# A three-stage float32 kernel: the experts' token tiles go from 512 to 768, and the MLP's output is prepared in single steps

## The chip, the cores and the metric

The kernel runs on one core of a Trainium2 chip. The metric is the device time of one execution in microseconds (us); smaller is better. The engines of the core are TensorE (PE, matrix products into PSUM, with weight loads listed apart as PEld), VectorE (DVE), ScalarE (ACT), GpSimd (POOL) and SyncE (SP), which here does nothing but issue the transfers (DMA) between DRAM and the on-chip buffer. TensorE's granted clock has two levels, 1.2 and 2.4 GHz; views write it as a share of full speed, 0.50 to 1.00.

## The reference

Three stages follow each other, on 4 x 576 = 2304 tokens of width 512:

```python
# 1: linear attention, 4 batches x 8 heads x 576 x 64, features of 128
proj = q_or_k @ w_phi;  proj -= max|proj|;  phi = concat(exp(proj), exp(-proj))
x = (phi_q @ (phi_k^T v)) / (phi_q . sum(phi_k) + 1e-6)      # -> 2304 x 512
# 2: MLP, 512 -> 2048 -> 512
h = x @ w_in
x = (h * clip(h + 3, 0, 6) / 6) @ w_out
# 3: eight experts, 512 -> 1024 -> 512, every token through every expert
P = exp(x @ w_gate - max); 8 times: P /= row sums; P /= column sums; P *= 2304 / 8
out = sum over e of P[:, e] * (relu(x @ w1[e]) @ w2[e])
```

## The kernel before, in words

**Number format.** A float32 operand is split into a rounded high half and the rest, the low half. A product is three matmuls into the same PSUM bank: high by high, low by high, high by low (`mm3`, lines 80 to 82). The two halves are made by one operation each: `hi_act` (ACT, line 67) and `lo_dve` (DVE, line 73), or `hi_pool` and `lo_pool` (POOL, lines 70 and 76).

**Order.** The program is written as Python generators that are advanced in turn. A scheduler in the framework then reorders the instructions within each engine when the kernel is built. Every engine runs its own list in order, and a wait for another engine or a transfer holds whatever stands behind it in that list. SP's list is that of all transfers.

**Attention and MLP.** The tokens are cut into chunks of 512, the last of 256. The MLP runs in four groups: chunks 0, 1 and 2 alone, then chunks 3 and 4 together. `mlp(g)` yields once for each step, and the attention of later batches is woven between the steps. In a step the first product goes to the bank `ps_h` (or `ps_kv` for chunk 4); ACT makes `t`, DVE makes `u`, ACT and DVE make the halves `gh` and `gl`, and the second product adds into the accumulators. Those are the banks `ps_acc`, and for chunk 4, whose 256 tokens need half as much, the two `ps_att` banks.

**The MLP's output.** Stage 3 multiplies its first layer by Strassen's scheme (seven products of half size in place of eight). The scheme's seven operands on the token side are `b11`, `b22`, `b21` (quarters of the transposed MLP output) and the differences `t1` to `t4`. When a group ends, `quarters()` copies the accumulators out (ACT, line 470, tile `xf`), makes four differences on POOL (line 476, tile `xt`), and `x_out()` makes the halves of each operand (tile `xo`, two buffers) and writes them to DRAM (line 463, `xs_...`). All of this stands at the end of the group in one piece. The buffers of `xf` and `xt` are those named `raw`, `t` and `u` of the pool `cv`, which the MLP's steps use too. Chunk 4 is not split in seven: its two operands `k1` and `k2` are read straight from `ps_att` by ACT and DVE.

**Experts.** A block is one expert and one half of its hidden layer; there are 16. For each block the five chunks pass through. A chunk of 512 takes the seven products in the order t1, b11, b22, t2, b21, t3, t4, each 4 x 3 matmuls of 256 columns in a half bank (`product`); the last chunk takes the full product, 48 matmuls of 256 columns. After a product ACT copies it (`kept`, line 785, tile `u`), or DVE adds a kept one to it (`plus`, line 789), and `relu_halves` makes the two halves of a hidden tile `h` (lines 762 and 763). `outputs()` is the second layer: 12 matmuls of 512 columns for each 128 tokens, of the chunk before, woven in by `PATTERN`. So a block has 4 x 84 + 48 = 384 matmuls of 256 columns and 18 x 12 = 216 of 512.

Operand tiles return from DRAM into `xr` (five buffers, asked for five products ahead by `x_ahead`, line 637). Expert weights land in `raw2` (8 buffers, lines 575 and 581), and POOL makes from them eight operands `w1o` a block (12 buffers) and four `w2o` (6 buffers). In views and in the order below the names are shortened: `raw` also stands for `raw2`, and all transfers of weights for `in_moe_w_dram`.

Of the kernel before, what the change touches and what calls it, by code (L numbers as in the profile page):

```python
# [21 lines left out]
def tile_kernel(ctx: ExitStack, tc, q, k, v, w_phi, w_in, w_out, w_gate, w1, w2, out):  # L22
# [81 lines left out]

    xctx = ctx.enter_context(ExitStack())
# [10 lines left out]
    def x_cols(c0, c1):  # L116
# [7 lines left out]
    HF = CH // 2  # L124
    XOPS = ("b11", "b21", "b22", "t4", "t1", "t2", "t3")
    xs = [
        {o: dram.tile([P, 4 * HF], F32, name="xs_%d_%s" % (ci, o)) for o in (XOPS if n == CH else ("k1", "k2"))}
        for ci, (_, n) in enumerate(chunks)
    ]
# [15 lines left out]
    def convert(dst, src):  # L145
        raw = cv.tile([P, DM, 2], I32, tag="raw", name="raw")
# [39 lines left out]
    xe = mctx.enter_context(tc.tile_pool(name="xe", bufs=1))  # L186
# [211 lines left out]
    def mlp(g):  # L398
# [60 lines left out]
    def x_out(ci, name, src):  # L459
        t = xe.tile([P, 2, 2, HF], F32R, tag="xo", name="xo", bufs=2)  # L460
        hi_act(t[:, 0], src)
        lo_dve(t[:, 1], src, t[:, 0])
        nc.sync.dma_start(xs[ci][name], f32(t).rearrange("p h k t -> p (h k t)"))

    def quarters(ci, o):
        q = []
        for h in range(2):
            f = cv.tile([P, 2, CH], F32, tag="raw", name="xf")
            for k in range(2):
                nc.scalar.copy(f[:, k], o[2 * h + k])  # L470
            q += [f[:, :, 0:HF], f[:, :, HF:]]
        b11, b12, b21, b22 = q

        def sub(a, b, tag):
            t = cv.tile([P, 2, HF], F32, tag=tag, name="xt")
            nc.gpsimd.tensor_tensor(out=t, in0=a, in1=b, op=ALU.subtract)
            return t

        t1 = sub(b12, b11, "t")
        t2 = sub(b22, t1, "u")  # L480
        for name, src in (("t1", t1), ("b11", b11), ("b22", b22), ("t2", t2), ("b21", b21)):
            x_out(ci, name, src)
        x_out(ci, "t3", sub(b22, b12, "t"))
        x_out(ci, "t4", sub(b21, t2, "u"))
# [84 lines left out]
    def w_load(b):  # L569
        e, j = blocks[b]  # L570
        for r in range(2):
            for k in range(2):
                t = wp.tile([P, 2, BF], F32, tag="raw2", name="raw2", bufs=8)
                src = w1[e, k * HF:(k + 1) * HF, r * FH + j * BF:r * FH + (j + 1) * BF]
                nc.sync.dma_start(t, src.rearrange("(k p) f -> p k f", p=P))
                raw[b, "a%d%d" % (r + 1, k + 1)] = t
        for r in range(2):
            for q in range(QB):
                t = wp.tile([P, DM], F32, tag="raw2", name="raw2", bufs=8)
                f0 = r * FH + j * BF + q * P  # L580
                nc.sync.dma_start(t, w2[e, f0:f0 + P, :])
                raw[b, r * QB + q] = t
# [8 lines left out]
    def w1_prep(b):  # L591
        a = {o: raw.pop((b, o)) for o in ("a11", "a12", "a21", "a22")}
# [6 lines left out]
        def keep(o, src):  # L599
            wops[b, o] = halves("w1o", 12, src)  # L600

        s1 = add(a["a21"], a["a22"], ALU.add)
        keep("s1", s1)
        s2 = add(s1, a["a11"], ALU.subtract)
        yield
        keep("s4", add(a["a12"], s2, ALU.subtract))
# [3 lines left out]
        keep("s3", add(a["a11"], a["a21"], ALU.subtract))  # L610
        yield
        for o in ("a11", "a12", "a22", "a21"):
            keep(o, a[o])
            yield

    def w2_prep(b):
        for i in range(2 * QB):
            w2t[b, i] = halves("w2o", 6, raw.pop((b, i)))
            yield
# [6 lines left out]
    ORDER = ("t1", "b11", "b22", "t2", "b21", "t3", "t4")  # L626
    WITH = {"t1": "s1", "b11": "a11", "b22": "s4", "t2": "s2", "b21": "a12", "t3": "s3", "t4": "a22"}
    units = [(b, c) for b in range(len(blocks)) for c in range(len(chunks))]
    wanted = [(c, o) for _, c in units for o in (ORDER if chunks[c][1] == CH else ("k1", "k2"))]
# [3 lines left out]
    def x_ahead(n):  # L633
        while len(xring) < min(n, len(wanted)):
            c, o = wanted[len(xring)]
            t = wp.tile([P, 2, 2, HF], F32R, tag="xr", name="xr", bufs=XR)
            nc.sync.dma_start(f32(t).rearrange("p h k t -> p (h k t)"), xs[c][o])
            xring.append(t)
# [3 lines left out]
    for g in range(len(groups)):  # L642
        im = 0
        s0, s1 = done_by((g + 1) * HP - 1) if g else 0, done_by((g + 2) * HP - 1)
        for _ in mlp(g):
            im += 1
            if g + 1 < B:
                upto(s0 + LEAD + (s1 - s0) * im // (4 * NFF + 1))
            elif im == 8:
                w_load(0)  # L650
                first = w1_prep(0)
            elif im % 8 == 0:
                take(first, 1)
            elif im == 120:
                x_ahead(XR - 1)
# [12 lines left out]
    mo = ctx.enter_context(tc.tile_pool(name="mo", bufs=1, reuse_waits="tile"))  # L668
    hp_ = ctx.enter_context(tc.tile_pool(name="hp", bufs=1, side="right", reuse_waits="tile"))
    acc = mo.tile([P, NTT, DM], F32, name="acc")  # L670
    take(w2_prep(0), 9)
    pm = mo.tile([P, NTT, E], F32, name="pm")

    def sinkhorn():
        r1 = mo.tile([P, NTT], F32, name="r1")
# [28 lines left out]
    def store(i):  # L704
        c = i * P
# [14 lines left out]
    gate_ps = []  # L720
# [210 lines left out]
```

## Time and profile before

| | |
|---|---|
| three timed runs | 2310.23, 2317.01, 2313.9 us; median 2313.9 us |
| profiled execution | 2309.93 us, of which the traced span is 2307.9 us |
| attention and MLP | 0 to about 741 us of the span |
| experts | about 741 us to the end |
| TensorE busy | 2227.2 us, 97% of the span |
| VectorE, ScalarE, GpSimd busy | 48%, 29%, 41% |
| mean granted TensorE clock | 0.988 |

Times are read from the span's start. "Busy" for an engine is the time in which one of its instructions ran. A row in brackets such as `[11.19 <-DVE xo L73]` says that the engine had been idle for 11.19 us and that the DVE instruction of line 73 writing `xo` ended this.

### The profile page before, as it was taken

What the parts mean: (1) busy time and instruction counts of PE and PEld (TensorE: products, weight loads), DVE (VectorE), ACT (ScalarE), POOL (GpSimd) and SP (SyncE); (2) the same over time, 40 slices, a digit from 0 to 9 for tenths busy, and PEclk for the clock granted to TensorE, in tenths of its full rate; (3) what the DMA queues carried; (4) which work ended last, traced back from release to release, by engine and by line L of the source; (5) the groups of instructions that cost most, each with busy time, mean ns of one, the idle gap of its engine ahead of it and who ended that gap; (6) DMA issues with size and microseconds to landing.
All of it is one profiled execution on the core that took longest, in us unless ns stands there. A gap on an engine that the chain in (4) does not pass through costs nothing.

```text
span 2307.9 us, 33330 instructions
## 1 busy us (share of the span) xinstructions
PE 2227.2 (97%) x13207; PEld 1952.3 (85%) x13207; DVE 1105.8 (48%) x1486; ACT 668.3 (29%) x1270; POOL 936.0 (41%) x895
## 2 busy tenths in 40 slices
PE   8899899899899899999999999999999999999999
PEld 6677677788688789899899999999989999899998
DVE  6899876666533215543333433334333343334433
ACT  5566555554322222111121111211112111121111
POOL 2565867776873131623315223142231422314100
PEclk9999999999899899999999999999999999999999
DMA  4354432321511646465465654656546555465464
GB/s 119 100 156 147 143 116 83 111 89 60 214 65 64 225 136 206 160 219 178 165 210 166 213 187 157 210 179 209 186 160 211 180 198 185 163 214 187 156 196 133
DMA packets 181258, 372.42 MB, mean 161 GB/s; under 512 B 70384, under 2 KB 95088, under 8 KB 181104
## 3 DMA queue, kind: packets, MB, share of 16 engines
q1 hardware_dynamic: 181104, 370.29, 48.2%
q8 instruction: 106, 1.74, 0.3%
q14 instruction: 48, 0.39, 0.1%
HBM read 341.39 MB, written 28.84 MB: 160 GB/s over the span
## 4 chain that ended last, share of the span: by engine, by line
PE 66%; DVE 1%; DMA 1%; ACT 0%; issue 0%; ACTq 0%
PE ps_acc L80 11%; PE ps_acc L81 11%; PE ps_acc L82 11%; PE ps_att L80 4%; PE ps_att L82 4%; PE ps_att L81 4%; PE ps_kv L80 3%; PE ps_kv L82 3%; PE ps_kv L81 3%; PE ps_h L80 3%; PE ps_h L82 3%; PE ps_h L81 3%; PE ps_acc L726 0%; DMA xs_b<-xo 0%; DMA xr<-xs_t 0%; PE ps_acc L738 0%
## 5 line engine op out<-in xcount | busy, mean ns | idle before, releaser
L80 PE MATMUL ps_acc<-w2o,h 128*128 128x512 f32 x1152 | 451.8, 392 | 0.0
L81 PE MATMUL ps_acc<-w2o,h 128*128 128x512 f32 x1152 | 451.6, 392 | 0.0
L82 PE MATMUL ps_acc<-w2o,h 128*128 128x512 f32 x1152 | 448.5, 389 | 0.0
L856 DVE SCALAR_TENSOR_TENSOR acc<-ps_acc,pm,acc 128x512 f32<-128x512 f32 x252 | 188.7, 749 | 432.5 <-PE ps_acc L82 431.3
L70 POOL TENSOR_SCALAR w1o<-raw 128x512 fp32r<-128x512 f32 x64 | 46.8, 731 | 646.8 <-PE ps_att L82 643.7
L82 PEld LDWEIGHTS ps_acc<-w2o,h 128*128 128x128 f32 x1152 | 216.6, 188 | 46.9
L80 PEld LDWEIGHTS ps_acc<-w2o,h 128*128 128x128 f32 x1152 | 217.3, 189 | 38.2
L81 PEld LDWEIGHTS ps_acc<-w2o,h 128*128 128x128 f32 x1152 | 217.4, 189 | 35.5
L80 PE MATMUL ps_att<-xr,w1o 128*128 128x256 f32 x768 | 219.1, 285 | 13.1 <-DVE xo L73 11.2
L762 ACT ACTIVATE h<-u 128x512 fp32r<-128x512 f32 x192 | 114.3, 627 | 373.0 <-DVE u L789 373.0
L763 DVE SCALAR_TENSOR_TENSOR h<-u,h 128x512 fp32r<-128x512 f32 x192 | 177.2, 950 | 89.9 <-ACT h L762 89.9
L82 PE MATMUL ps_att<-xr,w1o 128*128 128x256 f32 x768 | 218.7, 285 | 0.0
L81 PE MATMUL ps_att<-xr,w1o 128*128 128x256 f32 x768 | 218.6, 285 | 0.0
L785 ACT COPY u<-ps_att 128x512 f32<-128x512 f32 x128 | 75.1, 587 | 428.8 <-PE ps_att L82 428.8
L80 PE MATMUL ps_kv<-xr,w1o 128*128 128x256 f32 x640 | 181.4, 283 | 0.0
L82 PE MATMUL ps_kv<-xr,w1o 128*128 128x256 f32 x640 | 181.3, 283 | 0.0
L80 PE MATMUL ps_h<-xr,w1o 128*128 128x256 f32 x640 | 181.3, 283 | 0.0
L82 PE MATMUL ps_h<-xr,w1o 128*128 128x256 f32 x640 | 181.3, 283 | 0.0
L81 PE MATMUL ps_h<-xr,w1o 128*128 128x256 f32 x640 | 181.3, 283 | 0.0
L81 PE MATMUL ps_kv<-xr,w1o 128*128 128x256 f32 x640 | 181.3, 283 | 0.0
L76 POOL TENSOR_TENSOR wl<-wf,wh 128x512 fp32r<-128x512 f32 x128 | 174.2, 1361 | 10.2
L80 PEld LDWEIGHTS ps_att<-xr,w1o 128*128 128x128 f32 x768 | 148.1, 193 | 19.5 <-DVE xo L73 11.5
(251 smaller groups left out, 4856.3 us busy)
## 6 DMA issues: line engine op xcount, KB each, us to landing
xr<-xs_t SPq DMA_DIRECT2D x256, 512.0 KB, 4.1
xr<-xs_b SPq DMA_DIRECT2D x192, 512.0 KB, 4.1
raw<-in_moe_w_dram SPq DMA_DIRECT2D x128, 256.0 KB, 3.5
wf<-scratch SPq DMA_DIRECT2D x48, 512.0 KB, 3.2
xr<-xs_k SPq DMA_DIRECT2D x32, 512.0 KB, 3.8
raw<-in_moe_w_in_dram SPq DMA_DIRECT2D x16, 512.0 KB, 3.7
raw<-in_moe_w_out_dram SPq DMA_DIRECT2D x16, 512.0 KB, 3.9
scratch<-wf SPq DMA_DIRECT2D x16, 512.0 KB, 3.1
```

What stands on the lines that cost most here:

```text
L70: nc.gpsimd.tensor_scalar(dst, src, 1.0, 1.0, op0=ALU.mult, op1=ALU.mult)
L76: nc.gpsimd.tensor_tensor(out=dst, in0=src, in1=f32(hi), op=ALU.subtract)
L80: nc.tensor.matmul(o, lhsT=wh, rhs=xh, start=start, stop=False, skip_group_check=chk)
L81: nc.tensor.matmul(o, lhsT=wh, rhs=xl, start=False, stop=False, skip_group_check=chk)
L82: nc.tensor.matmul(o, lhsT=wl, rhs=xh, start=False, stop=stop, skip_group_check=chk)
L762: nc.scalar.activation(t[:, 0], src, AF.Relu)
L763: nc.vector.scalar_tensor_tensor(out=t[:, 1], in0=src, scalar=0.0, in1=f32(t[:, 0]), op0=ALU.max, op1=ALU.subtract)
L785: nc.scalar.copy(t, ps)
L856: nc.vector.scalar_tensor_tensor(out=a, in0=ps, scalar=pm[:, ti, e:e + 1], in1=a, op0=ALU.mult, op1=ALU.add)
```

## The change

**Units.** The experts take the tokens in three units of 768. Of the unit's six tiles of 128 the even ones are one half of Strassen's token side and the odd ones the other. Each of the seven products has two parts, and a part is 6 matmuls of 384 columns in a bank of its own (both `ps_att` banks, or `ps_h` and `ps_kv`). The last 256 tokens are now part of the third unit, and the special case for them (`hidden_last`, `k1`, `k2`) is gone. One `outputs()` follows each of the first six products. A block has 3 x 84 = 252 matmuls of 384 columns and 216 of 512. The gate's matmuls in the first block become 60 of 384 columns instead of 88 of 256.

**The MLP's output.** `operands()` replaces `quarters()` and `x_out()`. At the end of a group it copies the accumulators out (two copies on ACT and two on DVE for a chunk, chunk 4 first) and stops. Each later step makes one operand: differences on DVE instead of POOL, the halves as before, the transfer out one step late and in pieces of one token tile. `make()` takes such a step at every third step of the next MLP group, and two at each part of a product in the first unit of the experts. The tiles lie in a pool `xe` of their own.

**Weights.** Seven `w1o` operands a block instead of eight, in 10 buffers instead of 12; `raw2` has 6 buffers instead of 8, and the loads for the first and the second layer are asked for apart. `h` gets 10 buffers (7 before), `u` 8 (6). The accumulator `acc` of the second layer is opened after the first unit.

```diff
-    HF = CH // 2
-    XOPS = ("b11", "b21", "b22", "t4", "t1", "t2", "t3")
...
+    HK = DM // 2
+    NUN = 3
+    UP = NTT // 2 // NUN
+    UW = UP * P
+    XOPS = ("t1", "b11", "b22", "t2", "b21", "t3", "t4")
+    xs = [{o: dram.tile([P, 4, UW], F32, name="xs_%d_%s" % (c, o)) for o in XOPS} for c in range(NUN)]
...
-        for ci in parts:
-            if chunks[ci][1] == CH:
-                quarters(ci, [rows(ci, dd)[0] for dd in range(KD)])
-            else:
-                for i, o in enumerate(("k1", "k2")):
-                    x_out(ci, o, acc[ci, i].rearrange("p (k t) -> p k t", k=2))
+        for ci in reversed(parts):
+            making.append(operands(ci, rows))
+            next(making[-1])
...
+    def operands(ci, rows):
+        c0, n = chunks[ci]
+        w = n // 2
+        q = {}
         for h in range(2):
-            f = cv.tile([P, 2, CH], F32, tag="raw", name="xf")
+            f = xe.tile([P, 2, 2, w], F32, tag="raw" if n == CH else "xl", name="xf")
             for k in range(2):
-                nc.scalar.copy(f[:, k], o[2 * h + k])
+                src = rows(ci, 2 * h + k)[0].rearrange("p (i s t) -> p s i t", s=2, t=P)
+                dst = f[:, k].rearrange("p s (i t) -> p s i t", t=P)
+                if k == 0:
+                    nc.scalar.copy(dst, src)
+                else:
+                    nc.vector.tensor_copy(dst, src)
...
+        def sub(a, b):
+            t = xe.tile([P, 2, w], F32, tag="xt", name="xt")
+            nc.vector.tensor_tensor(out=t, in0=a, in1=b, op=ALU.subtract)
...
+            t = xe.tile([P, 2, 2, w], F32R, tag="xo", name="xo")
+            hi_act(t[:, 0], q[o])
+            lo_dve(t[:, 1], q[o], t[:, 0])
+            if last is not None:
+                out_(*last)
+            last = o, t
+            yield
...
+    def make(n=1):
+        while n and making:
+            if next(making[0], 1):
+                making.pop(0)
+            n -= 1
...
-                t = wp.tile([P, 2, BF], F32, tag="raw2", name="raw2", bufs=8)
+                t = wp.tile([P, 2 * BF], F32, tag="raw2", name="raw2", bufs=6)
...
-            wops[b, o] = halves("w1o", 12, src)
+            wops[b, o] = halves("w1o", 10, src)
...
             im += 1
+            if im % 3 == 0:
+                make()
...
-    UB, HB = 6, 7
+    UB, HB = 8, 10
...
-    def product(ps, w, x, fresh):
-        for q in range(QB):
-            qs = slice(q * P, (q + 1) * P)
-            o = ps[:, q * HF:(q + 1) * HF]
-            for k in range(2):
-                mm3(o, w[:, 0, k, qs], w[:, 1, k, qs], x[:, 0, k, :], x[:, 1, k, :], fresh and q == 0 and k == 0, True, True)
+    def product(ps, w, x, q, fresh):
+        qs = slice(q * P, (q + 1) * P)
+        for k in range(2):
+            mm3(ps, w[:, 0, k, qs], w[:, 1, k, qs], x[:, 0, k, :], x[:, 1, k, :], fresh and k == 0, True, True)
...
+        for i, o in enumerate(XOPS):
+            x_ahead(n0 + i + XR)
+            x = xring[n0 + i]
             for q in range(QB):
...
+                if o in ("t1", "b21"):
+                    X[q] = bank("att")[:, 0:UW]
+                if o == "b11":
+                    A[q] = bank(("h", "kv")[q])[:, 0:UW]
+                ps = (X if o in ("t1", "b22", "b21") else A)[q]
+                product(ps, wops[b, WITH[o]], x, q, o in ("t1", "b11", "b21"))
...
-    PATTERN = {(7, 0): "UUUUUUU", (7, 4): "UUDUUDUUDUD", (7, 2): "UUDUUUUDU", (2, 4): "UDDUDD"}
...
+        for i, _ in enumerate(hidden(b, c, n0, got)):
+            if not out_pool:
+                make(2)
+            if i % QB == QB - 1 and behind:
                 outputs(*behind.pop(0))
-        n0 += steps
+        if not out_pool:
+            make(99)
+            ectx.close()
+            mo = ctx.enter_context(tc.tile_pool(name="mo", bufs=1, reuse_waits="tile"))
+            out_pool += [mo, mo.tile([P, NTT, DM], F32, name="acc"), mo.tile([P, NTT, E], F32, name="pm")]
+            take(w2_prep(0), 9)
...
         if c == 0:
-            if late is not None:
-                take(late, 2)
+            if b > 0:
+                take(late, 9)
             if b + 1 < len(blocks):
-                w_load(b + 1)
-                coming = w1_prep(b + 1)
-                late = w2_prep(b + 1)
...
-            take(coming, {0: 1, 1: 2, 2: 1, 3: 5, 4: 0}[c])
-            take(late, {1: 1, 2: 1}.get(c, 0))
+                w_load(b + 1, False)
+                coming, late = w1_prep(b + 1), w2_prep(b + 1)
+        if b + 1 < len(blocks):
+            take(coming, (1, 3, 9)[c])
+            if c == 1:
+                w_load(b + 1, True)
+            take(late, (0, 0, 2)[c])
```

How the change moves instructions is seen in three places; lines with - are of the order before, lines with + of the changed one, each a run of instructions as they stand on the engine.

ACT where the MLP's last group ends and the experts begin (`gh` is the last MLP step's, `xf` the copied accumulators, `xo` the operands, `u` the kept products). Before:

```order
L67 ACTIVATE gh<-u 128x256
L470 COPY xf<-ps_acc 128x512 x3
L67 ACTIVATE xo<-xt 128x512
L470 COPY xf<-ps_acc 128x512
L67 ACTIVATE xo<-xf 128x512 x2
L67 ACTIVATE xo<-xt 128x512
L67 ACTIVATE xo<-xf 128x512
L67 ACTIVATE xo<-xt 128x512 x2
L67 ACTIVATE xo<-ps_att 128x512 x2
L785 COPY u<-ps_att 128x512
```

The banks `ps_att` are read last, after all operands of chunk 3. In the changed kernel the same place reads:

```order
L67 ACTIVATE gh<-u 128x256
L472 COPY xf<-ps_acc 128x512 x2
L472 COPY xf<-ps_att 128x256 x2
L67 ACTIVATE xo<-xt 128x256
L67 ACTIVATE xo<-xf 128x256
L804 COPY u<-ps_att 128x384 x2
L804 COPY u<-ps_h 128x384
L67 ACTIVATE xo<-xf 128x256
```

Four copies stand in front of the experts' first work, and the operands are spread behind it.

ACT where the third MLP group ends and the fourth begins (`t` and `gh` are of the new group's steps). Before:

```order
L470 COPY xf<-ps_acc 128x512 x3
L67 ACTIVATE xo<-xt 128x512
L470 COPY xf<-ps_acc 128x512
L67 ACTIVATE xo<-xf 128x512
L436 ACTIVATE t<-ps_h,cst 128x512
L67 ACTIVATE xo<-xf 128x512
L67 ACTIVATE xo<-xt 128x512
L67 ACTIVATE gh<-u 128x512
L436 ACTIVATE t<-ps_kv,cst 128x256
L67 ACTIVATE xo<-xf 128x512
L67 ACTIVATE gh<-u 128x256
```

Every `xo` among these waits for one of two buffers. In the changed kernel:

```order
L472 COPY xf<-ps_acc 128x512 x2
L67 ACTIVATE xo<-xt 128x512
L67 ACTIVATE xo<-xf 128x512
L439 ACTIVATE t<-ps_h,cst 128x512
L439 ACTIVATE t<-ps_kv,cst 128x256
L67 ACTIVATE gh<-u 128x512
L67 ACTIVATE xo<-xf 128x512
L67 ACTIVATE gh<-u 128x256
L67 ACTIVATE xo<-xt 128x512
```

Two operands still stand ahead of the first `t` here, and the others come one or two between the steps.

SP's transfers in the middle of the experts' stage, around the weights of one block (`xr` are operand tiles; the number after `xs_b` or `xs_t` is the operand's). Before:

```order
L637 DMA xr<-xs_t_100 128x1024
L581 DMA raw_9401<-in_moe_w_dram 128x512
L581 DMA raw_9403<-in_moe_w_dram 128x512
L575 DMA raw_10267<-in_moe_w_dram 128x2x256
L637 DMA xr<-xs_b_96 128x1024
L637 DMA xr<-xs_t_101 128x1024
L637 DMA xr<-xs_t_98 128x1024
L575 DMA raw_10269<-in_moe_w_dram 128x2x256
```

In the changed kernel:

```order
L669 DMA xr<-xs_t_101 128x1536
L608 DMA raw_9480<-in_moe_w_dram 128x512
L608 DMA raw_9482<-in_moe_w_dram 128x512
L611 DMA raw_9979<-in_moe_w_dram 128x2x256
L611 DMA raw_9981<-in_moe_w_dram 128x2x256
L669 DMA xr<-xs_b_102 128x1536
```

Four weight loads instead of three now stand together ahead of an operand tile.

## Rows read from the trace of the kernel before

**Rows 1.** The page's head.

```profile
span 2307.9 us, 33330 instructions
```

**Rows 2.** Stretches: length, busy us (instructions) of five engines, clock, DMA share, GB/s.

```profile
276.00:300.00 24.00, 18.11 (x90) 14.05 (x89) 17.19 (x22) 13.31 (x28) 14.68 (x15) 0.93 0.52 173
440.00:466.00 26.00, 20.77 (x99) 16.00 (x98) 18.40 (x24) 15.25 (x30) 18.16 (x16) 0.93 0.47 178
587.00:622.00 35.00, 23.80 (x105) 19.84 (x104) 17.74 (x16) 10.85 (x20) 33.99 (x30) 0.76 0.61 222
741.00:765.00 24.00, 12.80 (x83) 11.83 (x82) 8.14 (x10) 7.20 (x13) 11.53 (x11) 0.72 0.70 263
765.00:2308.00 1543.00, 1535.01 (x9663) 1390.12 (x9663) 593.46 (x829) 295.71 (x501) 441.06 (x426) 1.00 0.55 184
595.00:605.30 10.30, 5.24 (x12) 4.15 (x13) 5.94 (x5) 2.41 (x5) 10.22 (x9) 0.50 0.04 15
612.10:619.00 6.90, 5.16 (x17) 4.46 (x18) 6.52 (x6) 2.72 (x6) 6.90 (x7) 0.51 0.67 254
748.60:762.30 13.70, 6.07 (x27) 5.97 (x28) 3.77 (x6) 4.16 (x7) 7.32 (x8) 0.50 0.63 231
```

**Rows 3.** Timeline of PE in the experts' stage: start, us, instruction.

```profile
1499.89 0.40 PE L80 MATMUL ps_acc<-w2o,h 128*128 128x512 f32 x1
...
1502.64 0.28 PE L80 MATMUL ps_att<-xr,w1o 128*128 128x256 f32 x1
...
1505.51 0.40 PE L80 MATMUL ps_acc<-w2o,h 128*128 128x512 f32 x1
```

**Rows 4.** Timeline of PE in the attention: matmuls of 288 columns.

```profile
293.26 0.29 PE L81 MATMUL ps_att<-El,kvh 128*128 128x288 f32 x1
...
293.79 0.29 PE L82 MATMUL ps_att<-Eh,kvl 128*128 128x288 f32 x1
```

**Rows 5.** Timeline of POOL over one block of the experts.

```profile
1498.70 0.62 POOL L70 TENSOR_SCALAR w1o<-raw 128x512 fp32r<-128x512 f32 x1 [38.38 <-PE ps_att L82]
...
1547.06 0.62 POOL L70 TENSOR_SCALAR w2o<-raw 128x512 fp32r<-128x512 f32 x1 [14.29 <-PE ps_acc L82]
...
1554.40 1.29 POOL L76 TENSOR_TENSOR w2o<-raw,w2o 128x512 fp32r<-128x512 f32 x1
1594.06 0.62 POOL L70 TENSOR_SCALAR w1o<-raw 128x512 fp32r<-128x512 f32 x1 [38.38 <-PE ps_att L82]
```

**Rows 6.** Costliest groups and DMA issues of the page (mean ns; us to landing).

```profile
L763 DVE SCALAR_TENSOR_TENSOR h<-u,h 128x512 fp32r<-128x512 f32 x192 | 177.2, 950 | 89.9 <-ACT h L762 89.9
L785 ACT COPY u<-ps_att 128x512 f32<-128x512 f32 x128 | 75.1, 587 | 428.8 <-PE ps_att L82 428.8
xr<-xs_t SPq DMA_DIRECT2D x256, 512.0 KB, 4.1
```

**Rows 7.** Timelines of ACT, DVE and SP's queue, third to fourth MLP group.

```profile
594.58 0.69 ACT L436 ACTIVATE t<-ps_h,cst 128x512 f32<-128x512 f32 x1 [3.40 <-POOL xt L476]
...
611.17 0.63 ACT L67 ACTIVATE xo<-xf 128x512 fp32r<-128x512 f32 x1 [10.14 <-DMA xs_b<-xo]
...
597.47 1.75 DVE L73 TENSOR_TENSOR xo<-xt,xo 128x512 fp32r<-128x512 f32 x1
...
605.71 0.32 SPq L168 DMA_DIRECT2D wf<-scratch  x1
606.12 0.39 SPq L463 DMA_DIRECT2D xs_b<-xo  x1
```

**Rows 8.** Timelines of DVE and PE where the experts begin.

```profile
755.48 0.69 DVE L73 TENSOR_TENSOR xo<-ps_att,xo 128x512 fp32r<-128x512 f32 x1 [0.65 <-ACT xo L67]
...
756.23 0.58 PE L80 MATMUL ps_att<-xr,w1o 128*128 128x256 f32 x1 [11.19 <-DVE xo L73]
```

**Rows 9.** What PE waited for between 587 and 622 us: total, times, longest.

```profile
PE ps_h L80 <- DVE u L438: 7.0, 1, 7.0
```

More of the change, by code (lines that the diff above doesn't have):

```diff
@@ L623, in take @@
             next(g, 0)
-    ORDER = ("t1", "b11", "b22", "t2", "b21", "t3", "t4")
     WITH = {"t1": "s1", "b11": "a11", "b22": "s4", "t2": "s2", "b21": "a12", "t3": "s3", "t4": "a22"}
-    units = [(b, c) for b in range(len(blocks)) for c in range(len(chunks))]
-    wanted = [(c, o) for _, c in units for o in (ORDER if chunks[c][1] == CH else ("k1", "k2"))]
+    units = [(b, c) for b in range(len(blocks)) for c in range(NUN)]
+    wanted = [(c, o) for _, c in units for o in XOPS]
     XR = 5
@@ L717, in store, with gate_add @@
             c += n
-    gate_ps = []
-    def gate_add(x, kh, tokens, first=False):
+    gate_ps = {}
+    def gate_add(x, kh, t):
+        first = t not in gate_ps
+        if first:
+            gate_ps[t] = bank("acc")
         for k in range(2):
             for h in range(2):
-                for t in tokens:
-                    nc.tensor.matmul(
-                        gate_ps[-1][0:2 * E, t * HF:(t + 1) * HF], lhsT=wg[:, 2 * kh + k, :], rhs=x[:, h, k, :],
-                        start=first and k == 0 and h == 0 and t == tokens[0], stop=True, skip_group_check=True,
-                    )
+                nc.tensor.matmul(
+                    gate_ps[t][0:2 * E, 0:UW], lhsT=wg[:, 2 * kh + k, :], rhs=x[:, h, k, :],
+                    start=first and k == 0 and h == 0, stop=True, skip_group_check=True,
+                )
@@ L731, in gate_end @@
     def gate_end(c):
-        c0, n = chunks[c]
-        lt = hp_.tile([2 * E, CH], F32, tag="u", name="lt", bufs=UB)
-        nc.scalar.copy(lt[:, 0:n], gate_ps.pop(0)[0:2 * E, 0:n])
+        lts = []
+        for t in range(2):
+            lts.append(hp_.tile([2 * E, UW], F32, tag="u", name="lt", bufs=UB))
+            nc.scalar.copy(lts[-1], gate_ps.pop(t)[0:2 * E, 0:UW])
         yield
-        ps = bank("acc")
-        for i in range(n // P):
-            nc.tensor.matmul(ps[:, i * E:(i + 1) * E], lhsT=lt[:, i * P:(i + 1) * P], rhs=sel, start=True, stop=True)
@@ L785, in kept, with plus @@
+        def kept(name, q, ps):
+            T[name, q] = t = hp_.tile([P, UW], F32, tag="u", name="u", bufs=UB)
             nc.scalar.copy(t, ps)
-            return t
-        def plus(t, ps):
+        def plus(name, q, ps):
+            t = T.pop((name, q))
             nc.vector.tensor_tensor(out=t, in0=ps, in1=t, op=ALU.add)
             return t
-        xp = bank("att")
-        step("t1", xp, True)
-        p5 = kept(xp)
-        yield
-        ap = a_bank()
-        step("b11", ap, True)
@@ L841, in outputs @@
+    def outputs(b, ti, hs, t):
+        _, acc, pm = out_pool
         e, j = blocks[b]
```

233 lines of the change are left out of this document (97 added, 136 removed).

## The prediction

> **What bounds the kernel now.** I read the stretches first. From 765 us to the end TensorE is busy 1535.01 of 1543 us at full clock; DVE, ACT and POOL have 593, 296 and 441 [rows 2]. So in the experts' stage only TensorE's own matmuls count, and a block is as long as their sum. POOL's pattern repeats after 1594.06 - 1498.70 = 95.36 us [rows 5]. The pace of the matmuls stands in [rows 3]: 12 of 512 columns from 1499.89 to 1502.64, 0.2292 us each (the 0.40 shown is latency, they overlap), then 24 of 256 to 1505.51, 0.1196 each. 384 x 0.1196 + 216 x 0.2292 = 45.9 + 49.5 = 95.4 us: a block is explained without any wait.
>
> In the MLP the losses stand where one group ends and the next begins. TensorE has idle time of 5.9 us in 276 to 300, 5.2 in 440 to 466, 11.2 in 587 to 622 and 11.2 in 741 to 765 (length less busy) [rows 2]. Around the last two the clock falls as well: 5.24 us of work in 595 to 605, 5.16 in 612 to 619 and 6.07 in 749 to 762 ran at 0.50 [rows 2], each time after TensorE had stood idle. At full speed that work takes half, so 2.6, 2.6 and 3.0 us are lost besides.
>
> Their causes. At 587, ACT's list holds the MLP's `t` and `gh` between the operands `xo`. `t` at 594.58 waited 3.40 us for POOL's `xt`, since they share buffers, and at 611.17 ACT had stood 10.14 us for a transfer out of `xo`: SP took that transfer only at 606.12, behind a weight load `wf` [rows 7]. TensorE's longest wait there, 7.0 us for `u`, follows from it [rows 9]. At 741 the first experts' product t1 needs a `ps_att` bank, and both hold chunk 4's result until DVE has made `k1` and `k2`; DVE's first of the two comes at 755.48 and TensorE starts at 756.23 after 11.19 us [rows 8].
>
> **A. 768-token units.** Per block, 384 matmuls of 256 columns become 252 of 384; the 216 of 512 stay. No row has 384 columns. Bounds: the slope from 256 to 288 columns ([rows 4]: four steps in 0.53 us, 0.1325 each, so 0.0129 for 32 columns) gives 0.1196 + 4 x 0.0129 = 0.171 us; time purely by column from the 256 rows gives 1.5 x 0.1196 = 0.179. The midpoint between 256 and 512 is 0.174, close to three quarters of the 512 row (0.172); I take 0.174, since both neighbours point there. 252 x 0.174 = 43.85 us, 2.08 less than 45.93; 16 blocks give **-33 us** (bounds -45 and -11.5). The gate moves from 88 x 256 to 60 x 384 columns, 22.5 against 23.0 thousand: nothing.
>
> What hides the rest of A. ACT and DVE get more, smaller instructions: 18 instead of 12 copies a block (0.587 each at 512 columns [rows 6]), and half as many again of the others. DVE had 593 of 1543 us [rows 2]; a half more is 890 against TensorE's 1500: covered. The narrowest chain is an A bank that DVE reads (`plus` after t3) before t4 adds into it: between lie the other part, 6 x 0.174 = 1.04 us, and an `outputs()`, 2.75 us, against one DVE operation of at most 0.95 [rows 6]. Without `outputs()`, in the first unit, this cover is about 1 us, and t4 may wait a microsecond or two: it is in B's remainder. An operand tile is 768 KB instead of 512; 21 a block instead of 30 make 15.75 MB instead of 15. With 184 GB/s of now [rows 2] in a shorter block that is about 200; 263 GB/s was reached [rows 2]. A tile is asked for four products ahead, 4 x (2 x 1.04 + 2.75) = 19 us in a unit with outputs; landing took 4.1 for 512 KB [rows 6], some 6 for 768.
>
> **B. Where the experts begin.** The 11.2 us of waiting and 3.0 of slow clock, 14.2 together, go if `ps_att` comes free at once. ACT's list now has four copies ahead of anything else, two of `ps_acc` and two of `ps_att`, with DVE doing the other half; by the 0.587 of a 512-wide copy [rows 6] all four, two of them half as wide, need about 2 us. What is late next: in unit 0 there are no `outputs()` to cover DVE, which makes operands between; and `acc` opens only when the last of these is out. I leave 3 us: **-11 us** (0 to -14).
>
> **C. Third to fourth group.** 11.2 + 2.6 + 2.6 = 16.4 us. `xe` has its own buffers, the differences are on DVE, and the transfers go out a step late, so neither the wait for `xt` nor the 10.14 us for `xo` has its cause any more. But two operands still stand ahead of the first `t` on ACT, and their low halves (1.75 us at worst [rows 7]) on DVE ahead of the first `u`; and POOL, busy 33.99 of 35 us here [rows 2], still makes all weights. I leave 4.4: **-12 us** (0 to -16).
>
> **D. First two boundaries.** 5.9 + 5.2 = 11.1 us. There attention steps are woven in, and part of the waits is theirs; I give the change half, **-6 us** (0 to -11).
>
> **Weights and buffers.** Seven instead of eight operands spare POOL about 1.9 us a block, which bounds nothing (441 of 1543 [rows 2]): 0. `raw2` with 6 buffers and four loads in one run ahead of an operand tile can hold SP: POOL's chain that frees them runs from 1547.06 to 1555.69, 8.6 us [rows 5], then one landing. That is under the 19 us ahead of use, so 0 here, and a rival below. The transfers out in smaller pieces are read back only later in unit 0 or after it: 0.
>
> **Sum.** -33 - 11 - 12 - 6 = -62 us. The profiled execution took 2309.9 us, 2 us more than its span [rows 1]; the median of the three runs shown is 4 us higher than it. 2309.9 - 62 = **2248 us**.
>
> **Rivals.**
> R1, the sum above: 2248.
> R2, the operands' work is only moved: ACT, DVE and SP do as much as before, and each step now queues ahead of some `t`, `u` or attention operation that TensorE waits for; a wait of a half microsecond at each of some 60 steps gives back B, C and D. For it: DVE has 17.19 of 24 us and 18.40 of 26 at the first two boundaries [rows 2], and gets the differences too. Against it: the waits named above have causes (bank, shared buffer, SP) that are gone. Half to all of 29 us given back, with A kept: 2262 to 2277, say 2272.
> R3, time goes by columns, and a matmul has hardly any fixed part: then A is worth -11.5, and the sum 2309.9 - 11.5 - 29 = 2269. Against it: 512 columns take 0.2292, not 2 x 0.1196 = 0.2392, and the step from 256 to 288 is 0.0129, not the 0.0150 of proportion [rows 3, 4].
> The Trainium skill, page "TensorE: Matmul & The Clock Gate", section "Back-to-back issue gap", speaks for R3: it gives the gap of a single matmul at full clock as N / 2.4 + 2.5 ns, so a fixed part of 2.5 ns. By that 256 columns take 109 ns and 384 162.5, and A would be 16 x (384 x 0.1092 - 252 x 0.1625) = 16 us, an estimate from the page. The trace has 119.6 and 229.2 ns where the page's formula gives 109 and 216, so about 13 ns each that it doesn't count, which is what A lives on. The section's other figure, 131 ns for sustained matmuls of 512 columns, is far below what this trace shows.
> R4, slower than before: SP stands at one of the four weight loads in a row, an operand tile behind it comes late, and TensorE waits once in each block. The gain of 62 us is used up at 62 / 15 = 4.1 us a block, that is when SP is held until 19 - 6 + 4.1 = 17 us; its nearest row is POOL's chain of 8.6 us plus one landing, about 12.6. For it: POOL stands up to 38.38 us for TensorE [rows 5], and a load behind such an operand would be held that long. Against: these loads' buffers hang on the `w2o` chain and not on that wait, and now TensorE never waits for POOL at all. At 8 us a block: 2309.9 - 62 + 120 = 2368.
> R5, the boundaries' gain comes but 0.3% or less is left: for that A would have to be near its smaller bound and R2 hold fully.
>
> **Chances.** R1 0.68, R2 0.13, R3 0.10, R4 0.07 (0.05 of it past the break-even), R5 0.02. A measurement of this kernel tells about 0.3%, 7 us, from no change (its three runs spread over 6.8). R1 to R3, and the small part of R4, are faster: 0.93; R5 is the same: 0.02; slower 0.05. The range: A to D all at their larger bounds give 2309.9 - 45 - 14 - 16 - 11 = 2224; at the other end R2 with all 29 given back is 2277, and with A a little small some 2285. From **2226 to 2284** it holds R1 to R3; it leaves out R4, R5 and the corners.
>
> **What would show it.** A: matmuls of 384 columns 0.174 us apart, a block of 93.3 us by POOL's or PE's repetition, PE still over 99% busy after the first unit. B: the first `ps_att` product starts within 3 us of the last MLP matmul, and no stretch at 0.50 there. C and D: the largest wait in each boundary under 3 us, none for `xo` transfers. Wrong would be: 0.179 a matmul (R3); many new waits of half a microsecond on `t`, `u` or `gh` between 276 and 740 (R2); PE waiting on `xr` or `w2o` once a block (R4).

## The result, and the profile after

The changed kernel takes 2258.91 us (median; 2255.77 to 2262.98), the kernel before 2313.19 (2310.23 to 2317.01) in the same comparison: a ratio of 0.9765, 95% interval 0.9743 to 0.9787, so 54 us less. 2248 were forecast, 2226 to 2284 as the range. The profiled execution took 2262.98 us, the slowest of its four, while the one shown of before (2309.93) was faster than all four timed here; between the two traces the difference is therefore only 46.9 us. The parts below are read from these two, with a second trace of the changed kernel (span 2254.0 us) beside them.

The page's head and the stretches that answer to [rows 1, 2] (columns as there):

```profile
span 2261.1 us, 29200 instructions
...
276.00:300.00 24.00, 22.01 (x115) 18.54 (x116) 22.02 (x28) 14.97 (x30) 14.24 (x15) 0.93 0.54 157
440.00:466.00 26.00, 22.64 (x124) 18.53 (x121) 24.60 (x30) 14.79 (x28) 16.77 (x14) 1.00 0.55 164
587.00:622.00 35.00, 28.14 (x143) 23.93 (x142) 23.13 (x25) 11.24 (x21) 34.67 (x31) 0.90 0.56 167
735.00:765.00 30.00, 25.81 (x130) 22.79 (x129) 15.99 (x31) 12.40 (x27) 0.02 (x1) 0.89 0.90 282
765.00:2261.00 1496.00, 1490.05 (x7438) 1339.60 (x7436) 651.33 (x1009) 330.72 (x678) 433.59 (x408) 1.00 0.56 196
```

TensorE is busier at every group end (22.01 of 24 us where it was 18.11, 28.14 of 35 where it was 23.80), and from 765 us on it is as full as before, at full clock. What TensorE still waits for, from 587 to 622 and from 735 to 765 us (total, times, longest):

```profile
PE ps_h L82 <- POOL wl L76: 2.6, 1, 2.6
PE ps_h L80 <- POOL wh L70: 2.4, 1, 2.4
PE ps_h L80 <- DVE u L441: 1.9, 1, 1.9
...
PE ps_att L80 <- DMA xr<-xs_t: 4.2, 1, 4.2
```

The 7.0 us of [rows 9] and the 11.19 us for the bank [rows 8] are gone; weights from POOL, one late `u` and a late operand tile are the waits now. One of 1.3 us for ACT's `h` follows before 800 us; after 800 us no wait is listed at all.

A block by POOL's repetition, and TensorE's pace, both in the experts' stage (answering to [rows 5, 3]):

```profile
1460.12 0.62 POOL L70 TENSOR_SCALAR w1o<-ws 128x512 fp32r<-128x512 f32 x1 [28.97 <-PE ps_att L82]
...
1553.96 0.62 POOL L70 TENSOR_SCALAR w1o<-ws 128x512 fp32r<-128x512 f32 x1 [28.96 <-PE ps_att L82]
```

```profile
1500.88 0.39 PE L80 MATMUL ps_acc<-w2o,h 128*128 128x512 f32 x1
...
1503.64 0.33 PE L80 MATMUL ps_h<-xr,w1o 128*128 128x384 f32 x1
...
1504.71 0.33 PE L80 MATMUL ps_kv<-xr,w1o 128*128 128x384 f32 x1
...
1505.75 0.39 PE L80 MATMUL ps_acc<-w2o,h 128*128 128x512 f32 x1
```

A block takes 93.84 us (before 95.36; forecast 93.35). The pace shows why it is not the forecast: six matmuls of 384 right behind an `outputs()` take 1503.64 to 1504.71, 178 ns each; the next six, 1504.71 to 1505.75, take 173. The twelve of 512 take 2.76 us, 230 ns each, where [rows 3] had 229.

Where the time came from, by the starts and ends of TensorE's work in the traces (us):

```
                                    before   changed  changed, 2nd  before_own_buffers
first MLP matmul                      74.9      75.7        75.6         74.8
first of the fourth group            588.7     584.0       579.6        586.1
  third of its sixteen steps         616.9     601.2       598.1        603.1
  ninth                              670.1     656.9       651.0        666.9
last MLP matmul                      741.1     727.8       722.0        737.9
first of the third block             962.6     926.0       918.7        954.1
last matmul                         2302.8    2255.9      2248.6       2294.3
```

The first three groups took 513.8 us and take 508.3, the fourth 152.3 and 143.9. The entry into the experts, from the last MLP matmul to the third block, was 221.5 us and is 198.2; less two steady blocks each (190.7 and 187.7) that leaves 30.8 and 10.5. But four `outputs()` fewer are done by then (30 against 34), 4 x 2.75 = 11.0 us that come later, so the entry gained 9.3 us. In the kernel with own buffers, tested below, the entry less two steady blocks leaves 25.5.

### The profile page after: what moved, and what is told of

Its sections match the earlier page's. It is cut to its first block, busy times and chain, and to the rows that moved or that the text cites. A ratio compares the mean times of both kernels' runs of the same rounds, so it can differ in the third digit from the quotient of the medians.

```text
span 2261.1 us, 29200 instructions
## 1 busy us (share of the span) xinstructions
PE 2198.0 (97%) x11067; PEld 1916.8 (85%) x11067; DVE 1191.0 (53%) x1714; ACT 707.9 (31%) x1462; POOL 896.7 (40%) x847
## 4 chain that ended last, share of the span: by engine, by line
PE 83%; DVE 8%; POOL 3%; issue 2%; ACT 2%; DMA 1%; SPq 0%; POOLq 0%; DVEq 0%; ACTq 0%
PE ps_acc L81 13%; PE ps_acc L82 13%; PE ps_acc L80 13%; PE ps_att L80 5%; PE ps_att L82 5%; PE ps_att L81 5%; PE ps_h L80 5%; PE ps_h L82 5%; PE ps_h L81 5%; PE ps_kv L80 3%; PE ps_kv L81 3%; PE ps_kv L82 3%; DVE dn L381 2%; POOL wf L163 1%; POOL wl L76 1%
## 5 line engine op out<-in xcount | busy, mean ns | idle before, releaser
L793 ACT ACTIVATE h<-u 128x384 fp32r<-128x384 f32 x288 | 140.6, 520 | 590.6 <-DVE u L808 590.6
L794 DVE SCALAR_TENSOR_TENSOR h<-u,h 128x384 fp32r<-128x384 f32 x288 | 237.8, 857 | 9.6
L70 POOL TENSOR_SCALAR w1o<-ws 128x512 fp32r<-128x512 f32 x64 | 44.2, 691 | 452.6 <-PE ps_att L82 451.2
L70 POOL TENSOR_SCALAR w2o<-raw 128x512 fp32r<-128x512 f32 x64 | 50.6, 800 | 383.9 <-PE ps_acc L82 378.5
L80 PE MATMUL ps_att<-xr,w1o 128*128 128x384 f32 x576 | 194.8, 338 | 5.5 <-DMA xr<-xs_t 4.2
L82 PE MATMUL ps_att<-xr,w1o 128*128 128x384 f32 x576 | 194.0, 337 | 0.0
L81 PE MATMUL ps_att<-xr,w1o 128*128 128x384 f32 x576 | 193.5, 336 | 0.0
L804 ACT COPY u<-ps_att 128x384 f32<-128x384 f32 x192 | 92.4, 481 | 228.2 <-PE ps_att L82 227.6
L70 POOL TENSOR_SCALAR wh<-wf 128x512 fp32r<-128x512 f32 x128 | 97.7, 763 | 113.8 <-PE ps_h L81 38.4
L80 PE MATMUL ps_h<-xr,w1o 128*128 128x384 f32 x384 | 131.6, 343 | 0.0
L82 PE MATMUL ps_h<-xr,w1o 128*128 128x384 f32 x384 | 131.1, 341 | 0.0
L81 PE MATMUL ps_h<-xr,w1o 128*128 128x384 f32 x384 | 130.0, 339 | 0.0
L80 PE MATMUL ps_kv<-xr,w1o 128*128 128x384 f32 x384 | 128.5, 335 | 0.0
L81 PE MATMUL ps_kv<-xr,w1o 128*128 128x384 f32 x384 | 128.5, 335 | 0.0
```

Source lines behind the costliest of these rows:

```text
L70: nc.gpsimd.tensor_scalar(dst, src, 1.0, 1.0, op0=ALU.mult, op1=ALU.mult)
L80: nc.tensor.matmul(o, lhsT=wh, rhs=xh, start=start, stop=False, skip_group_check=chk)
L81: nc.tensor.matmul(o, lhsT=wh, rhs=xl, start=False, stop=False, skip_group_check=chk)
L82: nc.tensor.matmul(o, lhsT=wl, rhs=xh, start=False, stop=stop, skip_group_check=chk)
L793: nc.scalar.activation(t[:, 0], src, AF.Relu)
L794: nc.vector.scalar_tensor_tensor(out=t[:, 1], in0=src, scalar=0.0, in1=f32(t[:, 0]), op0=ALU.max, op1=ALU.subtract)
```

## The experiments

Each was timed in five rounds beside the kernel before, whose median was 2312 us each time; every ratio is to it.

**The changed kernel again.**

> The changed kernel unchanged, beside the three others. Its first trace shows a block of 93.84 us against 95.36 before, a wait of 4.2 us in the experts' first unit, and waits of 1.9, 2.4 and 2.6 us between 587 and 622. Expected of this run: the same within 4 us, 2255 to 2263 us.

2257.97 us, ratio 0.9759 (0.9742 to 0.9776). The spread of single runs, 2252.6 to 2261.0, is wider than that of most other versions. Of the 7.1 us between the spans of the two traces, 4.3 arise in the first three groups, and it was not followed up where; 1.5 arise in the fourth. There, between 602 and 609 us the first trace has the clock at 0.59:

```profile
602.00:609.00 7.00, 4.51 (x11) 3.59 (x12) 1.32 (x1) 0.00 (x0) 7.00 (x8) 0.59 0.53 158
```

TensorE had waited 2.41 and 2.60 us for POOL's weights, within four microseconds. In the second trace the waits for POOL at this place are 1.41 us at the longest, and the matmuls of 512 columns stay at 0.23 us instead of 0.43.

**Two `outputs()` in a row.**

```diff
-            if i % QB == QB - 1 and behind:
+            if i % (2 * QB) == 2 * QB - 1 and behind:
                 outputs(*behind.pop(0))
+                outputs(*behind.pop(0))
```

> Two outputs() after every second product instead of one after each. Theory: what the predicted 33 us of the units lost to 24 is paid each time the width of the matmuls changes. In the changed kernel's trace the six matmuls of 384 columns behind an outputs() take 177.6 ns each and all others 173.3; the twelve of 512 behind a product take 230.1, where the kernel before, in the few places with two outputs() in a row, shows 226.7 for the second. Then half the changes save 9 x (6 x 4.3 + 12 x 3.4) ns = 0.6 us a block, about 9 us in all, a block of 93.24 us; in the trace the second outputs() of a pair shows 226.7. Rival 1: the slow matmuls come from ScalarE and VectorE reading the finished product beside them; the reading stays, and so does the time (0, a block of 93.84). Rival 2: the hidden tiles come too late when two outputs() are missing behind a product, and TensorE waits: more than 93.84 a block.

2250.43 us, ratio 0.9727 (0.9714 to 0.9741), 7.5 less than the changed kernel. Its block and its pace:

```profile
1452.89 0.62 POOL L70 TENSOR_SCALAR w1o<-ws 128x512 fp32r<-128x512 f32 x1 [29.66 <-PE ps_att L82]
...
1546.12 0.62 POOL L70 TENSOR_SCALAR w1o<-ws 128x512 fp32r<-128x512 f32 x1 [29.68 <-PE ps_att L82]
```

```profile
1500.94 0.33 PE L80 MATMUL ps_att<-xr,w1o 128*128 128x384 f32 x1
...
1502.01 0.33 PE L80 MATMUL ps_att<-xr,w1o 128*128 128x384 f32 x1
...
1505.13 0.39 PE L80 MATMUL ps_acc<-w2o,h 128*128 128x512 f32 x1
...
1507.89 0.39 PE L80 MATMUL ps_acc<-w2o,h 128*128 128x512 f32 x1
...
1510.61 0.33 PE L80 MATMUL ps_h<-xr,w1o 128*128 128x384 f32 x1
```

93.23 us a block, as worked out. Behind a change of width six matmuls of 384 take 1.07 us, and the eighteen after them 3.12, 173 ns each; the first twelve of 512 take 2.76 us, the second twelve 2.72, 227 ns each. ScalarE and VectorE read the same finished products as before, so the rival that blamed them falls; and no new wait came.

With the width the operands and the banks change too. That these need not cost anything by themselves can be seen in the changed kernel's first trace where the fourth MLP group begins: one product of 512 columns follows another with other operands and another bank:

```profile
583.74 0.39 PE L82 MATMUL ps_acc<-gh,wl 128*128 128x512 f32 x1
583.97 0.39 PE L80 MATMUL ps_h<-xhi,wh 128*128 128x512 f32 x1
...
586.69 0.28 PE L80 MATMUL ps_kv<-xhi,wh 128*128 128x256 f32 x1
```

The twelve from 583.97 to 586.69 us take 2.72 us, 227 ns each from the first on.

**Three in a row.**

```diff
-            if i % QB == QB - 1 and behind:
-                outputs(*behind.pop(0))
+            if i in (5, 11) and behind:
+                for _ in range(3):
+                    outputs(*behind.pop(0))
```

> Three outputs() after the third and three after the sixth product of a unit. Theory: each pair of width changes costs 65 ns (26 for the six matmuls of 384 behind it, 39 for the twelve of 512); pairs saved nine of eighteen a block and made it 93.24 us as worked out; triples save twelve, so 93.06 us a block and 2 to 3 us less than pairs. Rival: three products in a row leave VectorE too little time before the accumulating bank is written again (2.1 us for a product of two parts against some 3 us of VectorE's and ScalarE's work on it), and TensorE waits in each unit: 93.3 us a block or more.

2248.39 us, ratio 0.9721 (0.9706 to 0.9736). POOL's repetition gives 1542.09 - 1449.05 = 93.04 us a block, where 93.06 was worked out:

```profile
1449.05 0.62 POOL L70 TENSOR_SCALAR w1o<-ws 128x512 fp32r<-128x512 f32 x1 [29.59 <-PE ps_att L82]
...
1542.09 0.62 POOL L70 TENSOR_SCALAR w1o<-ws 128x512 fp32r<-128x512 f32 x1 [29.60 <-PE ps_att L82]
```

A fixed cost for each pair of changes fits three points (18, 9 and 6 pairs a block: 93.84, 93.23, 93.04). VectorE kept up: three products in a row caused no wait in the steady blocks.

**All steps of the operands at once.**

```diff
             next(making[-1])
+        make(99)
         yield
```

> All steps of the operands are taken at once where a group ends, as before the change; buffers, engines and units are the changed kernel's. Theory: what removed the waits at the group ends is that the operands have their own buffers and that the banks are copied out first; the scheduler spreads the work itself, so that the time stays within 3 us of the changed kernel. Rival: the spreading does it, and most of the gain of the group ends, some 10 to 13 us, is lost again.

2259.38 us, ratio 0.9766 (0.9752 to 0.978): the same as the changed kernel. Taking the steps one by one in the code is worth nothing that can be measured. But this does not test whether spreading matters on the chip: the scheduler spreads the instructions in either case. In the two traces POOL's order is the same throughout, and ACT's where the fourth group begins, with the operands between the steps in both.

**Own buffers alone, in the kernel before.**

```diff
-        t = xe.tile([P, 2, 2, HF], F32R, tag="xo", name="xo", bufs=2)
+        t = xe.tile([P, 2, 2, HF], F32R, tag="xo", name="xo", bufs=3)
...
-            t = cv.tile([P, 2, HF], F32, tag=tag, name="xt")
+            t = xe.tile([P, 2, HF], F32, tag="x" + tag, name="xt", bufs=2)
```

> The kernel before, with the differences xt in buffers of their own (two of each tag) and three instead of two buffers of xo; the order of the code is unchanged. Theory: the waits between 587 and 622 come from shared and too few buffers, so that 8 to 14 of the 16.4 us there go, and 0 to 6 at the two earlier group ends: 2290 to 2306 us. Rival: it needs the work spread in steps or the differences off GpSimd, and the time stays within 4 us of before.

2301.17 us, ratio 0.9955 (0.9943 to 0.9968): 11 less than before. The time is within what the theory expected, but it was not gained at the expected place. The table above shows the inside: the first two steps of the fourth group take 17.0 us instead of 28.2, as good as the changed kernel's 17.2. But the next six take 63.8 us instead of 53.2, and the gain at this place is almost lost again (0.6 us remain of the fourth group's). TensorE waits there, from 600 to 680 us, for weights:

```profile
PE ps_h L80 <- POOL wh L70: 6.8, 3, 3.9
PE ps_h L82 <- POOL wl L76: 3.3, 4, 1.7
```

POOL makes as much as ever and is now the one that is late. In the changed kernel the same six steps take 55.7 us, and there POOL makes far fewer of the experts' operands `w1o` in them: 9.38 us of its time instead of 20.92 (the row's length, then the busy us of PE, PEld and POOL in instructions on `w1o`; first own buffers, then the changed kernel):

```profile
603.10:666.90 63.80, 0.00 (x0) 0.00 (x0) 20.92 (x22) 0.92 0.38 137
601.20:656.90 55.70, 0.00 (x0) 0.00 (x0) 9.38 (x9) 0.94 0.48 166
```

Most of what own buffers gave lies in the entry, 5.3 us (30.8 to 25.5), where the wait for the bank became shorter, and 2.5 us in the first three groups:

```profile
PE ps_att L80 <- DVE xo L73: 7.6, 1, 7.6
```

**Differences on POOL, in the changed kernel.**

```diff
-            nc.vector.tensor_tensor(out=t, in0=a, in1=b, op=ALU.subtract)
+            nc.gpsimd.tensor_tensor(out=t, in0=a, in1=b, op=ALU.subtract)
```

> The changed kernel with the differences of the operands back on GpSimd. Theory: VectorE's list is what the MLP's u waits in and GpSimd is the one that is full between 587 and 622 (34.67 of 35 us busy, and TensorE waits 2.4 and 2.6 us for its weights there): four differences of 1.3 us more on it make this stretch 3 to 6 us longer, and the first two group ends stay within 2 us. Rival: GpSimd has the time elsewhere, and moving them changes less than 2 us.

2263.57 us, ratio 0.9791 (0.9774 to 0.9808), some 5 us more than the changed kernel, with intervals that overlap a little. Its profiled execution took 2259.0 us, the fastest of its four and no more than the changed kernel's median, so its trace cannot show the whole loss; it does not show it where it was expected: from 580 to 622 us the waits for POOL are those of the changed kernel,

```profile
PE ps_h L80 <- POOL wh L70: 2.3, 1, 2.3
PE ps_h L82 <- POOL wl L76: 1.9, 1, 1.9
PE ps_h L80 <- DVE u L441: 0.2, 1, 0.2
```

and the fourth group takes 141.9 us. Where the 5 us arise stays open.

**Chunk 4 first, in the kernel before**, alone; with own buffers; and with GpSimd's queue for the transfers out.

```diff
-        for ci in parts:
+        for ci in reversed(parts):
             if chunks[ci][1] == CH:
                 quarters(ci, [rows(ci, dd)[0] for dd in range(KD)])
```

> The kernel before, with chunk 4's two operands made ahead of chunk 3's seven, and nothing else changed. Theory: the 11.2 us for which the experts' first product waited come from the two ps_att banks alone, and 3.0 us of slow clock from that wait; 10 to 14 us less than before, and the first product starts within 4 us of the last MLP matmul. Rival: the operands of chunk 3, now later, or the two buffers of xo, become what the next product waits for, and less than half of it comes.

2312.6 us, ratio 1.0004 (0.9995 to 1.0013): nothing, so the rival was right. The wait for the bank is gone, and others stand in its place:

```profile
759.50 1.01 PE L726 MATMUL ps_acc<-xr,wg 128*16 128x256 f32 x4 [9.12 <-DMA xr<-xs_t]
762.24 0.58 PE L80 MATMUL ps_att<-xr,w1o 128*128 128x256 f32 x1 [1.73 <-ACT u L785]
772.66 0.39 PE L80 MATMUL ps_h<-xr,w1o 128*128 128x256 f32 x1 [2.12 <-DMA xr<-xs_b]
```

> The kernel before with both edits of the two runs above: own buffers for xt, three of xo, and chunk 4 first; units of 512, differences on GpSimd, work in one piece. Theory: the two gains add (20 to 28 us less than before), and what is then left to the changed kernel, about 25 to 33 us, is the units of 768. Rival: one wait covers the other, and together they give no more than the larger alone.

2306.33 us, ratio 0.9972 (0.9961 to 0.9982): 6 less than before, but less than own buffers alone gave, so the two gains do not add. The changed kernel is 48 us below this version, twice what its units give (24 us, below); the rest of it was not tested apart. In the entry TensorE waits for ScalarE's copy of a product, and then for a tile:

```profile
752.73 0.58 PE L80 MATMUL ps_att<-xr,w1o 128*128 128x256 f32 x1 [5.89 <-ACT u L785]
...
761.92 0.55 PE L80 MATMUL ps_att<-xr,w1o 128*128 128x256 f32 x1 [4.43 <-DMA xr<-xs_t]
```

> The kernel before with chunk 4's operands first, and the transfers out of chunks 3 and 4 issued by GpSimd. With the banks free early TensorE waited 9.1 us for an operand tile instead of 11.2 for the bank. Theory: that tile's load stood in SyncE's list behind transfers out that wait for VectorE; on their own queue it comes in time, the 9.1 us go and 2 us of slow clock with them: 8 to 12 us less than before. Rival: ScalarE's and VectorE's lists, full of chunk 3's seven operands in one piece, are the next wait, and less than 4 us comes.

```diff
-        nc.sync.dma_start(xs[ci][name], f32(t).rearrange("p h k t -> p (h k t)"))
+        (nc.gpsimd if ci >= 3 else nc.sync).dma_start(xs[ci][name], f32(t).rearrange("p h k t -> p (h k t)"))
```

2318.89 us, ratio 1.0028 (1.0019 to 1.0037): slower. The wait for the tile fell only to 5.50 us, and the one for ScalarE's `u` rose to 11.49:

```profile
752.79 1.01 PE L726 MATMUL ps_acc<-xr,wg 128*16 128x256 f32 x4 [5.50 <-DMA xr<-xs_t]
765.30 0.58 PE L80 MATMUL ps_att<-xr,w1o 128*128 128x256 f32 x1 [11.49 <-ACT u L785]
```

So the kernel before had several waits one behind the other here, and taking out the first alone gave nothing.

**The transfers out on GpSimd's queue, in the changed kernel** (the same edit of its `out_`, for chunks 3 and 4).

> The transfers out of chunks 3 and 4's operands are issued by GpSimd instead of SyncE. Theory: the 4.2 us wait in the experts' first unit comes from SyncE's list, in which the load of the next unit's first operand tile stands behind two transfers out that wait for VectorE; with them on another queue the load is issued when its buffer comes free, the wait goes, and the slow clock behind it (15 matmuls at 0.32 instead of 0.17 us, 2.2 us): 6 us less. Rival: the transfers themselves are the limit there (the DMA share is 0.90 at 282 GB/s between 735 and 765), and the wait stays within 1.5 us of 4.2.

2276.97 us, ratio 0.9844 (0.9829 to 0.9859): 19 more than the changed kernel. In the changed kernel's first trace SP takes the load of the late tile only behind a transfer out, and TensorE starts with it 7.2 us later; from 735 to 742 us the transfers out in SP's list waited 3.4 us for DVE's `xo`:

```profile
740.76 0.51 SPq L487 DMA_DIRECT2D xs_t<-xo  x1
741.36 0.58 SPq L669 DMA_DIRECT2D xr<-xs_t  x1
...
748.58 0.66 PE L80 MATMUL ps_att<-xr,w1o 128*128 128x384 f32 x1 [4.19 <-DMA xr<-xs_t]
...
SPq L487 <- DVE xo L73: 3.4, 2, 1.8
```

With the transfers out on another queue the wait for the tile is gone, which agrees with the theory that the load was held up in SP's list; but TensorE is late there for other reasons, so that this alone is no proof. The transfers out now land after 5.7 us, instead of 3.4 for all of the changed kernel's (view of DMA issues):

```profile
xs_t<-xo POOLq DMA_DIRECT2D x12, 256.0 KB, 5.7
```

The operands are done later: the last transfer out is issued at 779.4 us instead of 769.4. That this follows from the two buffers of `xo` was not tested. TensorE waits for ScalarE, VectorE and the opening of `acc` (724 to 800 us, clock 0.82):

```profile
PE ps_acc L776 <- ACT acc L854: 7.0, 1, 7.0
PE ps_h L80 <- DVE u L808: 4.3, 2, 3.7
PE ps_att L80 <- ACT u L804: 4.1, 1, 4.1
```

**Six operand buffers**, with pairs and with triples.

```diff
-    XR = 5
+    XR = 6
```

> pairs, with six instead of five buffers for operand tiles, so that each is asked for one product earlier. Theory: the wait of 4.2 us in the experts' first unit is a load held up in SyncE's list behind transfers out that wait for VectorE; one product more (2.1 us) ahead takes at least half of it, and the clock stays at 1.00: 2 to 6 us less than pairs; the steady blocks stay at 93.24. Rival: the loads then come in each other's way (0.90 busy there) and the wait only moves: within 1.5 us of pairs.

2246.62 us, ratio 0.9714 (0.9702 to 0.9727), 3.8 less than pairs; the intervals overlap, but the trace agrees. The waits for operand tiles (3.7 and 1.1 us in pairs) are gone, and one of 2.2 us for VectorE is left:

```profile
PE ps_h L80 <- DVE u L808: 2.2, 1, 2.2
```

> triples with six operand buffers. Theory: what the two edits save lies in different places, 0.2 us in each steady block (93.04 against 93.24) and the load's wait in the first unit, so that they add: 3 us less than pairs with six buffers, 2242 to 2246 us, with no wait for an operand tile. Rival: in the first units the missing outputs() between the products bring back a wait of 2 us for VectorE, and the time is within 1.5 us of pairs with six buffers.

2244.65 us, ratio 0.9704 (0.9691 to 0.9717): 2.0 less than pairs with six, inside what was expected, and 13 less than the changed kernel. It is the fastest version here.

## Why the prediction was right, and where its sizes were off

Direction and range held. By the number alone 2258.91 lies as near to R3 (2269) as to R1 (2248); it is the traces that speak for R1, with 173 ns a matmul and the group ends shorter. Between the two traces the four terms came out so (forecast, measured): A -33, -24.3 (16 blocks of 95.36 and 93.84 us); B -11, -9.3; C -12, -8.5; D -6, -5.5. The MLP began 0.8 us later. The second trace of the changed kernel has -10.7, -10.0 and -9.8 for B, C and D, so each of these moves by up to a few microseconds from run to run.

**A** is the term that was mis-sized, by 8.7 us, and the cause is shown. The 384-column matmul was priced at 0.174 us and takes 0.1733 in a row of its like. What the sum left out is what a change of width costs: some 30 ns for the six matmuls of 384 behind it (1.07 us instead of 1.04) and 40 for the twelve of 512 (2.76 instead of 2.72), by the blocks of `triples` (93.84 - 93.04) / 12 = 67 ns a pair, so 1.2 us a block for 18 pairs. Before, with 256, a pair cost about 20 ns by the same timelines: twelve of 512 took 2.746 us and, right behind another twelve, 2.720, while twelve of 256 behind them were 7 ns shorter than others. Of [rows 3] I took 0.2292 and 0.1196, averages with such a change in them, and carried the 512 over unchanged. `pairs` and `triples` confirm this to 0.02 us a block. (The sum held 252 x 0.174 = 43.85 and 49.5 us; with the changes of width it is 44.1 and 49.7.)

**R3** is wrong as a price: 173 ns and not 179.
The formula of the Trainium skill ("TensorE: Matmul & The Clock Gate", "Back-to-back issue gap") had, as an estimate, 162.5 ns for 384 columns and 16 us for A; the trace does not agree, with 173 ns in a row and 24 us. It gives no cost for a change of width.

**B** had about the right size, but not by the reason given. The step that failed is "The 11.2 us of waiting and 3.0 of slow clock go if `ps_att` comes free at once": done alone that gave nothing. Behind the bank stood a load held in SP's list behind transfers out, and ScalarE's and VectorE's lists full of operands. The sum had put such transfers at 0, and counted a tile as asked for 19 us ahead; that is with `outputs()`, and in the first unit, without them, the same four products are 4 x 2.08 = 8.3 us. Of these waits the changed kernel kept 4.2 us (SP held the load until 741.36), with the clock at 0.50 for 5 us after, some 2.2 us more; that is twice the 3 us left over, which were meant for a wait for VectorE and not for a transfer. So of the two signs for B one held (the first `ps_att` product starts at 728.30 us, 0.5 behind the start of the last MLP matmul) and one did not (a stretch at 0.50 was there). What in the change made the entry shorter was not separated: own buffers alone gave 5.3 us there in the kernel before, and smaller operands of chunk 4, longer products to hide the load, and the order of the copies came at once. The price of the slow clock was a little high as well: before, matmuls of 256 columns took 0.214 us at 0.50 against 0.120 at full clock, so that the 6.07 us cost 2.7 and not 3.0.

**C** was right in its cause: own buffers alone bring the first two steps from 28.2 to 17.0 us. That they don't keep it without some relief of POOL was half seen ("POOL still makes all weights") and not priced. In the changed kernel POOL has less of the experts' weights to make at this place (9.38 us of `w1o` for 20.92). Whether the later start of these weights or the seven instead of eight operands does more was not separated; the differences on DVE are not needed for it (the fourth group took 141.9 us with them on POOL, in an execution of 2259.0 us). Writing the work in steps is not needed either, since the built order hardly changes (`in_one_piece`); what spreading on the engines is worth was not tested.

**D** came out near the forecast, -5.5 and -9.8 in the two traces, by a share that I had only chosen: that is luck. It counts the whole first three groups, and no run looked into their ends.

**R2** did not occur: TensorE is busier at each group end, and from 276 to 727 us TensorE waits three times for the MLP's `u` and `gl`, 3.0 us together, not dozens of times. **R4** did not either: no wait is listed after 800 us, with four loads in a row ahead of a tile.

## What to carry to other kernels

When matmul widths alternate, price the change of width as well as the matmul, and read both from a stretch in which several of a kind stand in a row; grouping like widths was worth 7.5 us here, 0.3% of the time. When a wait is to be removed, ask which other lists are late at the same moment: the first of several waits hides the others, and its length is no bound for the gain. And where a framework schedules, compare the built order before a rearrangement of the code gets credit, or is called useless.

## What the runs showed of the hardware that was not expected

At full clock the spacing of matmuls depends on what was ahead: 512 columns take 227 ns in a row and 230 on average over the first twelve behind 384; 384 take 173 and 178 over the first six behind 512. The same cost, 67 ns a pair, explains the steady blocks of three kernels (18, 9 and 6 pairs). That ScalarE's or VectorE's reading causes it is excluded by `pairs`, and a change of operands and bank at the same width cost nothing where it could be read (227 ns each from 583.97 us on in the changed kernel). Why a change of width costs is not settled here, and it is not the only thing that spaces the matmuls: in the same trace twelve of 512 columns take 2.81 us from 575.45 to 578.26, 234 ns each, without a change of width among them.
